# Two spectral filters and a gate in one kernel: weights in freed groups, eight turn buffers, a shorter first fold, and a new order

## The chip, the cores and the metric

The kernel runs on one core of a Trainium2 chip. The metric is the device time of one execution in microseconds, the median of three runs; lower is better. The profile comes from one execution, whose own time is given beside its span.

## The reference

x is 2048 x 1024 in bf16. Two filters work on the same x, each with its own complex weights of 2048 x 513, and a gate per row mixes them:

```python
def reference(A_x, A_w_r, A_w_i, B_x, B_w_r, B_w_i, gate_w):
    # S, D = 2048, 1024
    g = sigmoid((A_x * gate_w).sum(-1, keepdims=True))
    X = rfft2(A_x.astype(float32), axes=(-2, -1))
    a = irfft2(X * (A_w_r + 1j * A_w_i), s=(S, D)).astype(bfloat16)
    b = irfft2(X * (B_w_r + 1j * B_w_i), s=(S, D)).astype(bfloat16)   # the same x
    return g * a + (1 - g) * b
```

B_x is not used. So there is one forward transform, two products with weights, two inverse transforms, and the mix.

## The kernel before

The transforms are written as matmuls with constant matrices. The 2048 rows are split as 128 x 16 (row = 16 n1 + n2), and row n2 of the 16 is one unit of the first and the last steps; the spectrum along the rows is split into 16 groups kg. The steps are:

- **Loads and folds.** x arrives in R1 (`xload`). VectorE folds each row of 1024 by its symmetries into R4. `full_fold` does both levels (a half-length sum and difference, then sum and difference with the reversed half); `half_fold` does one level, and TensorE does the other by accumulating two matmuls, the second with F or with -F (the constant FN).
- **s1(n2)**: the matmuls along n1 with F, 128 columns each. The result is evicted from PSUM to R3 (`evZ`).
- **d(kg), s2(kg), s2x(kg)**: the transform along the 1024 with the constant DM, evicted to QR (`evQ`); then the 16-point step with S2, evicted to XR (`evX`, `evX5`). QR has three slots and XR has four (`NX`).
- **prod(b, m)**: on VectorE, the complex product of X for kg 2m and 2m+1 with the weights of filter b (0 is A, 1 is B), in one of three product tiles. Two instructions multiply (2056 elements each), two instructions combine in place (1028 elements each). For a product named in `DIRECT` the combining instructions are left out, and TensorE combines instead, with four more matmuls for each kg.
- **i1(b, kg)**: the inverse 16-point step with KI, evicted to a buffer of VT (`evV`). Then GpSimd issues a DMA from the VT buffer to R1 (A) or R4 (B), the **turn**, that moves data across partitions; 32 turns in all. The VT buffer comes free when the turn has landed. There are `NV` = 4 buffers. The gate uses parts of VT first, and i1 comes only after `gspec`, the last matmul of the gate's column sum.
- **gmm/gm(c)**: the gate's sigmoid, mixed into the constants of the inverse (RM becomes RA and RB).
- **s1i(n2), di(n2), un(n2), st(n2)**: the inverse along n1 of both filters at once, which needs all 32 turns; eviction `evU`; the inverse along the 1024 with DI; eviction `evo`; four unfold instructions on VectorE; a store.

Each filter's weights are loaded by `wload` in parts of groups kg into WB, which has room for 28 groups (16 of A and 12 of B). The last four groups of B go where A's first four were, after products (0,0) and (0,1). All loads and stores are issued by SP, in one order. Every weight load is written as overwriting the pad columns (`over(["wpad"])`), which the products read, so it waits for the products that were written before it.

The order on every engine is set when the kernel is built. `run` holds lists of units (class `U`), keeps an estimate of when each engine is free and each operand ready (class `Sched`), and takes at each step the unit that can begin first; among those that begin within 40 ns of it, the lowest `prio`. The class waits by semaphores for what is read and overwritten. An eviction goes to ScalarE or VectorE, whichever would end first, with `BIAS` ns in favour of ScalarE when VectorE has other work soon:

```python
ca, cd = 200 + 0.833 * n, 180 + 1.04 * n
ta, td = S.ready("act", self.reads, w), S.ready("dve", self.reads, w)
return (ta, "act", ca) if ta + ca <= td + cd + (BIAS if dnext[0] < td + 400 else 0) else (td, "dve", cd)
```

Of the kernel before, what the change touches and what calls it, by code (L numbers as in the profile page):

```python
# [4 lines left out]
dt = mybir.dt  # L5
# [5 lines left out]
NS = 514  # L11
NX = 4
QUEUE = 2500.0
NV = 4
DIRECT = ((1, 7),)
BIAS = 1200
# [10 lines left out]
def make_consts():  # L27
# [17 lines left out]
    C["FN"] = -C["F"]  # L45
# [89 lines left out]
class Sched:  # L135
# [23 lines left out]
    def op(self, eng, fns, reads=(), writes=(), dma=False, ns=0.0):  # L159
        if not isinstance(fns, (list, tuple)):  # L160
            fns = [fns]
        t0 = self.ready(eng, reads, writes)
        o = Op(eng, len(self.q[eng]), list(fns), dma, len(self.all))
        self.q[eng].append(o)
        self.all.append(o)
        for k in reads:
            assert k in self.writer, k
            o.deps |= self.writer[k]
            o.raw |= self.writer[k]
        for k in writes:  # L170
            if k[0] == "over":
                k = k[1]
            o.deps |= self.writer.get(k, set())
            o.deps |= self.readers.get(k, set())
        writes = [k for k in writes if k[0] != "over"]
        for k in reads:
            self.readers.setdefault(k, set()).add(o)
        for k in writes:
            self.writer[k] = {o}
            self.readers[k] = set()  # L180
        o.deps.discard(o)
        if dma:
            self.free[eng] = t0 + 600 * len(fns)
            self.dmafree = max(self.dmafree, t0) + ns
            o.end = max(self.free[eng], self.dmafree) + 2000
        else:
            self.free[eng] = o.end = t0 + ns
        return o
# [78 lines left out]
def bass_gated_mix__spectral_gfnet__spectral_gfnet__prompt_kernel(  # L267
# [17 lines left out]
    WB = sb("WB", 28 * 2 * NS)  # L285
# [41 lines left out]
    def tt(o, a, b, op):  # L327
        n = int(np.prod(o.shape[1:]))
        return (lambda e: e.tensor_tensor(out=o, in0=a, in1=b, op=op)), 150 + 0.523 * n  # L329
# [9 lines left out]
    class U:  # L339
        def __init__(self, name, eng, ops, reads=(), writes=(), after=(), then=(), prio=5, slot=False, can=None, dma=None):  # L340
            self.name, self.eng, self.ops, self.reads, self.writes = name, eng, ops, list(reads), list(writes)
            self.after, self.then, self.prio, self.slot, self.can, self.dma = after, then, prio, slot, can, dma

        def start(self):

            if any(a not in done for a in self.after) or (self.can and not self.can()):
                return None
            w = self.writes
            if self.eng == "pe" and "m7" in w and mown[0]:
                return None  # L350
            if self.slot:
                best = None
                for s, o in enumerate(psown):
                    if o is None:
                        t = S.ready(self.eng, self.reads, w + [("ps", s)])
                        if best is None or t < best[0]:
                            best = (t, self.eng, s)
                return best
            if self.eng == "ev":
                n = self.n  # L360
                ca, cd = 200 + 0.833 * n, 180 + 1.04 * n
                ta, td = S.ready("act", self.reads, w), S.ready("dve", self.reads, w)
                return (ta, "act", ca) if ta + ca <= td + cd + (BIAS if dnext[0] < td + 400 else 0) else (td, "dve", cd)
            return (S.ready(self.eng, self.reads, w), self.eng, None)
# [50 lines left out]
    def run(streams):  # L415
        streams = [list(s) for s in streams]
        while True:
# [13 lines left out]
            t0 = min(c[0][0] for c in cand)  # L431
            r, u, s = min((c for c in cand if c[0][0] <= t0 + 40), key=lambda c: (c[1].prio, c[0][0]))
# [11 lines left out]

    def xload(a, b):
        return U(("ldx", a), "sp", [(ap(R1, a * 1024, [[1024, b - a], [1, 1024]]), xv[:, a:b, :])], [],
                 [("x", i) for i in range(a, b)], dma=(True, 655.0 * (b - a)))

    def wcol(b, kg):
        return (16 * b + kg) % 28 * 2 * NS  # L450
# [23 lines left out]
    def wload(b, ka, kb, j, c, g0=0, g1=16):  # L474
        key = ("W", b, ka, j, c, g0)
        for k in range(ka, kb):
            wkeys.setdefault((b, k), []).append(key)
        late = (b, ka) == (1, 12)
        u = U(("ldw", key), "sp", wpiece(b, ka, kb, j, c, g0, g1), [], [key] + over(["wpad"] + (wkeys[0, 0] if late else [])),
                 after=[("prod", 0, 0), ("prod", 0, 1)] if late else [], dma=(True, WNS * (kb - ka) * (g1 - g0) / 16.0), prio=6)  # L480
        if b and ka:
            base = u.start

            def start():
                r = base()
                return r and (max(r[0], S.dmafree - QUEUE), r[1], r[2])
            u.start = start
        return u
# [17 lines left out]
    loads = [xload(0, 2), cload("sp", FM, "F", 2048), xload(2, 4), cload("sp", FM, "FN", 2048, at=2048), xload(4, 8), xload(8, 12), xload(12, 16)]  # L506
    w = wseq([(0, 0, 8), (1, 0, 8), (0, 8, 16)], True)
    loads += w[:6] + [cload("sp", DM, "DM", 2048)] + w[6:8] + [cload("sp", S2, "S2", 768)] + w[8:18]
    loads += [cload("sp", KI, "KI", 1280), cload("sp", GS, "GS", 16)] + w[18:] + wseq([(1, 8, 12), (1, 12, 16)])
    lastload = [cload("sp", QR, "DI", 2048, over([("Q", r) for r in range(3)]), after=[("s2", 15), ("s2x", 15)])]  # L510
    midload = [cload("sp", WB, "RM", 2048, over(wkeys[0, 4] + ["wpad"]), after=[("prod", 0, 2)], at=8 * NS)]
# [18 lines left out]
    PEF = (4, 5, 6, 7, 8, 9, 10, 11)  # L530

    def half_fold(n2):

        rd = [("x", n2 + i) for i in range(4)]
        ops = []
        for i, op in enumerate((ALU.add, ALU.subtract)):
            for h in range(2):
                lo = ap(R1, n2 * 1024 + 256 * h, [[1024, 4], [1, 256]])
                hi = ap(R1, n2 * 1024 + 512 + 256 * h, [[1024, 4], [1, 256]])
                o = ap(R4, n2 * 1024 + 512 * i + (511 if h else 0), [[1024, 4], [-1 if h else 1, 256]])  # L540
                ops.append((tt(o, lo, hi, op), rd, [("u", n2 + k, 2 * i + h) for k in range(4)]))
        return U(("fold", n2), "dve", ops, rd, [("u", n2, 0)], after=[("ldx", n2)])

    def full_fold(n2):
        return fold(("fold", n2), 2, R1, n2 * 1024, TR, n2 // 2 % 2 * 2048, R4, n2 * 1024, 0, 128, [("x", n2), ("x", n2 + 1)],
                    ("st", n2 // 2 % 2), [("u", n2), ("u", n2 + 1)], after=[("ldx", {14: 12}.get(n2, n2))])

    folds = [full_fold(0), full_fold(2), half_fold(4), half_fold(8), full_fold(12), full_fold(14)]
    gfold = [fold("gfold", 1, TR, GO, TR, GO + 1024, TR, GO + 2048, 0, 1, ["gw"], ("gst",), [("ug",)], eng="pool", after=[("ld", "gw")])]

    def s1(n2):
        def ops(s):
            r = []
            for q in range(8):
                g, h = q // 2, q % 2
                o, f = pslot(s, q * 128, [[1, 128]]), ap(FM, n2 * 128, [[1, 128]])
                if n2 not in PEF:
                    r.append(mm(o, ap(R4, n2 * 1024 + q * 128, [[1, 128]]), f))
                else:

                    b = n2 * 1024 + g % 2 * 512 + h * 128
                    r.append(mm(o, ap(R4, b, [[1, 128]]), f, True, False))
                    r.append(mm(o, ap(R4, b + 256, [[1, 128]]), f if g < 2 else ap(FM, 2048 + n2 * 128, [[1, 128]]), False, True))
            return r
        return U(("s1", n2), "pe", ops, [("u", n2, i) for i in range(4 if n2 in PEF else 2)] + ["F"] + ["FN"] * (n2 in PEF),
                 after=[("fold", n2 // 4 * 4 if n2 in PEF else n2 // 2 * 2), ("ld", "F"), ("ld", "FN")], slot=True, prio=2,
                 then=[lambda s: EV(("evZ", n2), 1024, ap(R3, n2 * 32, [[512, 32], [1, 32]]), pslot(s, 0, [[32, 32], [1, 32]]),
                                    [], [("Z", n2)], slot=s)])

    def gate_row(c):  # L570

        ops = [mm(ap(PS, 32 * t * 4096 + 7 * 512, [[1, 512]], 0, 32), ap(VT, 2048 + (4 * r + t) * 32, [[1, 32]]),
                  ap(R3, (4 * r + t) * 2048 + c * 128, [[512, 4], [1, 128]]), r == 0, r == 1, 32 * t)
# [18 lines left out]
    allu = [("u", m, i) for m in range(16) for i in range(4 if m in PEF else 2)]  # L592
# [3 lines left out]
    def stage_d(kg):  # L596
        def ops(s):
            return [mm(pslot(s, o, [[1, 256]]), ap(R3, (2 * g + h) * 2048 + kg // 4 * 512 + kg % 4, [[4, 128]]),
# [36 lines left out]
    def prod(b, m):  # L635
# [6 lines left out]
        old = over([("st", i, t) for i in range(2) for t in "ST"] + ["gwt", "F", "FN"])  # L642
# [33 lines left out]
    def stage_i1(b, kg):  # L676
# [22 lines left out]
        def follow(s):  # L699
# [4 lines left out]
            def start():  # L704
                best = None
                for i in range(NV):
                    if vt[i] is None:
                        ev.writes = [("vt", i)] + zr
# [6 lines left out]
            def emit(st):  # L715
# [3 lines left out]
                ev.writes = [("vt", i)] + zr  # L719
# [15 lines left out]
        u = U(("i1", b, kg), "pe", ops, [], after=[("prod", b, kg // 2), "gspec"], can=can,  # L735
# [3 lines left out]
    def gmix(c):  # L739

        ops = [mm(misc(i * 128, [[1, 128]]), ap(ZG, 4 * c + i, [[0, 128]]), ap(WB, 8 * NS + (4 * c + i) * 128, [[1, 128]]))
               for i in range(4)]
        rm = ap(WB, 8 * NS + c * 512, [[1, 512]])
# [23 lines left out]
    def stage_dinv(n2):  # L767
        def ops(s):
            res = []

            for q, o in ((0, 0), (1, 256), (3, 512), (2, 768)):
                for h in range(2):
# [23 lines left out]
                               for t, n, k in ((WB, 56, "wpad"), (XR, 2 * NX, "xpad"))], [], ["wpad"])]  # L796
    run([pads, loads, midload, lastload, aloads, folds, gfold, gate, [s1(n) for n in R16], [stage_d(k) for k in R16], [stage_s2(k) for k in R16],
# [32 lines left out]
```

## Time and profile before

| | |
|---|---|
| median of 3 runs (lowest, highest) | 160.59 us (160.21, 160.77) |
| profiled execution | 159.51 us, span 157.7 us |
| mean granted TensorE clock | 0.941 |
| TensorE busy (1000 matmuls) | 115.1 us, 73% |
| VectorE busy | 114.3 us, 72% |
| ScalarE busy | 102.8 us, 65% |
| GpSimd busy | 25.4 us, 16% |
| moved by DMA | 28.52 MB, mean 181 GB/s |

The span runs from the first to the last instruction; the time of the same execution is 1.8 us longer. Busy times of different engines overlap, so they don't add up. In a group's row the columns are: line, engine, operation, output <- input, shapes and count; then busy time in us and the mean ns of one; then the idle time of the engine just before these instructions, and what ended it. Line 324 is the helper that makes every matmul, line 329 makes every VectorE operation on two tensors, line 374 is an eviction on ScalarE, 376 one on VectorE, and 369 is every DMA, so groups are told apart by their tiles and shapes.

### The profile page before, as it was taken

How to read it: one execution, taken by the hardware profiler on the slowest of the kernel's cores; microseconds unless marked ns; L12 is line 12 of the kernel's file. 1: busy time of each engine (PE TensorE's matmuls, PEld its weight loads, DVE VectorE, ACT ScalarE, POOL GpSimd, SP SyncE). 2: the span in 40 equal slices, each digit the busy share in tenths (PEclk: the TensorE clock that was granted, in tenths of full speed). 3: DMA queues.
4: the chain of work that ended last, by engine and by line, in shares of the span. 5: the costliest groups of instructions: out<-in, count | busy, mean ns of one | idle time of the engine just before them, and what ended most of it. 6: DMA issues, size and time to landing. Idle time of an engine off the chain costs nothing.

```text
span 157.7 us, 2620 instructions
## 1 busy us (share of the span) xinstructions
PE 115.1 (73%) x1000; PEld 79.4 (50%) x1008; DVE 114.3 (72%) x177; ACT 102.8 (65%) x113; POOL 25.4 (16%) x43
## 2 busy tenths in 40 slices
PE   0067999799739747999989964564905999999930
PEld 0054997766413214473635631122305999999920
DVE  0889875469975929399989978995220098998983
ACT  3045599586356526888899994572630688998960
POOL 6900000000003411422404131332310000000000
PEclk9999999999996975999999999999995699999997
DMA  5899999999765897567877857835551005343443
GB/s 151 298 434 422 267 264 244 237 238 217 203 173 117 198 247 142 143 160 194 183 172 153 203 134 186 243 77 152 116 137 50 0 11 192 112 157 137 155 182 133
DMA packets 18478, 28.52 MB, mean 181 GB/s; under 512 B 4641, under 2 KB 12961, under 8 KB 18082
## 3 DMA queue, kind: packets, MB, share of 16 engines
q1 hardware_dynamic: 13712, 19.95, 43.4%
q0 software_dynamic: 4608, 8.41, 23.2%
q8 instruction: 8, 0.13, 0.4%
q14 instruction: 4, 0.03, 0.1%
q10 hardware_dynamic: 146, 0.00, 0.1%
HBM read 15.75 MB, written 4.19 MB: 126 GB/s over the span
## 4 chain that ended last, share of the span: by engine, by line
PE 35%; DMA 21%; DVE 19%; ACT 17%; issue 5%; SPq 1%; DVEq 0%; POOL 0%; ACTq 0%; POOLq 0%
PE PS L324 35%; DMA R<-VT 15%; DVE TR L329 12%; ACT R L374 6%; ACT VT L374 6%; DMA WB<-in_B_w_i_dram 3%; DVE R L329 3%; DMA R<-in_A_x_dram 2%; ACT QR L374 2%; ACT XR L374 2%; DVE FM L329 2%; DVE XR L376 1%; SPq L369 1%; ACT GROW L374 1%; DVE R L376 1%
## 5 line engine op out<-in xcount | busy, mean ns | idle before, releaser
L374 ACT ACTIVATE R<-PS 128x1024 bf16<-128x1024 f32 x43 | 40.8, 1046 | 19.7 <-PE PS L324 19.6
L374 ACT ACTIVATE VT<-PS 128x1024 bf16<-128x1024 f32 (+1 forms) x34 | 32.9, 987 | 18.1 <-DMA R<-VT 14.1
L324 PE MATMUL PS<-TR,KI 128*128 128x512 bf16 x123 | 33.5, 411 | 15.1 <-ACT VT L374 8.4
L329 DVE TENSOR_TENSOR TR<-XR,WB 128x2056 bf16<-128x2056 bf16 x30 | 35.5, 1224 | 8.6 <-PE PS L324 6.1
L324 PE MATMUL PS<-DM,R 128*128 128x256 bf16 (+1 forms) x256 | 33.6, 260 | 1.8 <-ACT VT L374 1.0
L369 POOL DMA_DIRECT2D R<-VT x32 | 19.3, 603 | 89.7 <-ACT VT L374 87.8
L324 PEld LDWEIGHTS PS<-DM,R 128*128 128x128 bf16 x256 | 27.6, 112 | 4.0 <-ACT VT L374 1.9
L329 DVE TENSOR_TENSOR R<-R 128x512 bf16<-128x512 bf16 (+1 forms) x72 | 28.3, 449 | 1.6 <-DMA R<-in_A_x_dram 0.6
L324 PEld LDWEIGHTS PS<-TR,KI 128*128 128x128 bf16 x128 | 11.4, 103 | 31.7 <-ACT VT L374 12.1
L324 PE MATMUL PS<-FM,R 128*128 128x128 bf16 x192 | 15.0, 253 | 9.3 <-DVE R L329 8.9
L324 PE MATMUL PS<-R 128*128 128x128 bf16 x128 | 17.3, 237 | 5.9 <-DMA R<-VT 5.9
L374 ACT ACTIVATE QR<-PS 128x1024 bf16<-128x1024 f32 x15 | 14.9, 1025 | 7.0 <-PE PS L324 7.0
L324 PEld LDWEIGHTS PS<-FM,R 128*128 128x128 bf16 x192 | 14.1, 116 | 10.6 <-DVE R L329 8.8
L324 PE MATMUL PS<-QR,S 128*128 128x511 bf16 (+2 forms) x93 | 16.6, 306 | 2.8 <-ACT VT L374 1.6
L329 DVE TENSOR_TENSOR TR<-TR 128x1028 bf16<-128x1028 bf16 x28 | 18.1, 687 | 0.0
L324 PEld LDWEIGHTS PS<-R 128*128 128x128 bf16 x128 | 13.7, 107 | 6.1 <-DMA R<-VT 6.0
L324 PE MATMUL PS<-QR,R 128*128 128x256 bf16 x128 | 15.0, 273 | 1.3 <-ACT R L374 1.3
L376 DVE CAST R<-PS 128x1024 bf16<-128x1024 f32 x5 | 6.1, 1225 | 12.9 <-PE PS L324 12.9
L324 PEld LDWEIGHTS PS<-QR,S 128*128 128x128 bf16 x96 | 8.5, 98 | 13.2 <-ACT VT L374 2.7
L374 ACT ACTIVATE XR<-PS 128x1024 bf16<-128x1024 f32 (+1 forms) x15 | 11.8, 805 | 4.2 <-DVE FM L329 3.1
L324 PEld LDWEIGHTS PS<-QR,R 128*128 128x128 bf16 x128 | 12.3, 99 | 2.8 <-ACT R L374 1.5
L376 DVE CAST XR<-PS 128x1024 bf16<-128x1024 f32 (+1 forms) x9 | 6.7, 753 | 4.1 <-PE PS L324 4.1
(29 smaller groups left out, 44.8 us busy)
## 6 DMA issues: line engine op xcount, KB each, us to landing
R<-VT POOLq DMA_DIRECT2D x32, 256.0 KB, 5.5
out_dram<-R SPq DMA_DIRECT2D x16, 256.0 KB, 2.0
R<-in_A_x_dram SPq DMA_DIRECT2D x3, 1024.0 KB, 11.4
WB<-in_A_w_r_dram SPq DMA_DIRECT2D x15, 128.2 KB, 4.0
WB<-in_A_w_i_dram SPq DMA_DIRECT2D x13, 128.2 KB, 9.7
WB<-in_B_w_r_dram SPq DMA_DIRECT2D x16, 64.1 KB, 5.2
WB<-in_B_w_i_dram SPq DMA_DIRECT2D x16, 64.1 KB, 4.4
R<-in_A_x_dram SPq DMA_DIRECT2D x2, 512.0 KB, 5.1
```

Source lines behind the costliest of these rows:

```text
L324: return ((lambda e: e.matmul(o, l, r, start=start, stop=stop, skip_group_check=True, **kw)), max(65.0, 0.42 * n) * (1 if tile is None els ...
L329: return (lambda e: e.tensor_tensor(out=o, in0=a, in1=b, op=op)), 150 + 0.523 * n
L369: S.op(eng, [lambda e, d=d, s=s: e.dma_start(d, s) for d, s in self.ops], self.reads, self.writes, dma=self.dma[0], ns=self.dma[1])
L374: S.op("act", lambda e: e.activation(o, i, f), self.reads, self.writes, ns=x)
L376: S.op("dve", lambda e: e.tensor_copy(o, i), self.reads, self.writes, ns=x)
```

## The change

- WB has room for 24 groups. B's groups 8 to 15 go where A's groups 0 to 7 were: 8 to 11 after products (0,0) and (0,1), 12 to 15 after (0,2) and (0,3). The constant RM goes where A's groups 8 and 9 were, after product (0,4), instead of 4 and 5 after (0,2). The hold on late weight loads (`QUEUE`) is taken out.
- VT has 8 buffers. i1 no longer waits for `gspec`; only the three buffers that the gate uses do.
- `DIRECT` has five products instead of one.
- Every row is folded by the new `half_fold`: two instructions that add and subtract the reversed half. In s1 the matmuls have 256 columns: the first of a pair uses F twice, the second F and -F side by side. -F is made from F on ScalarE (`fneg`) instead of loaded.
- F is loaded in two parts, x in eight loads instead of five, and DM and S2 come ahead of all weights.
- The planner's costs, its window (200 instead of 40 ns, within one engine), its priorities (`PRIO`) and `BIAS` (0) are others, and a turn counts as landing 4.2 us after its transfer instead of 2.0.

The diff, cut to its core:

```diff
-QUEUE = 2500.0
-NV = 4
-DIRECT = ((1, 7),)
-BIAS = 1200
+NV = 8
+BIAS = 0
+WIN = 200
+DIRECT = ((0, 1), (1, 6), (1, 1), (0, 7), (1, 4))
+XCH = (0, 1, 2, 4, 6, 8, 12, 14, 16)
+PRIO = {'evU': 6, 'ldw': 2.5, 'gm': 2, 'fold': 0, 'evg': 4, 'evQ': 2.5, 'prod1': 6, 'evV1': 2.5, 's1': 3, 'i11': 1, 's2x': 2, 'di': 3, 'gspec': 1}
...
-    C["FN"] = -C["F"]
...
-            o.end = max(self.free[eng], self.dmafree) + 2000
+            o.end = max(self.free[eng], self.dmafree) + (4200 if eng == "pool" else 2000)
...
-    WB = sb("WB", 28 * 2 * NS)
+    WB = sb("WB", 24 * 2 * NS)
...
-        return (lambda e: e.tensor_tensor(out=o, in0=a, in1=b, op=op)), 150 + 0.523 * n
+        return (lambda e: e.tensor_tensor(out=o, in0=a, in1=b, op=op)), 110 + 0.521 * n
...
-                ca, cd = 200 + 0.833 * n, 180 + 1.04 * n
+                ca, cd = 180 + 0.825 * n, 160 + 1.04 * n
...
-            t0 = min(c[0][0] for c in cand)
-            r, u, s = min((c for c in cand if c[0][0] <= t0 + 40), key=lambda c: (c[1].prio, c[0][0]))
+            t0, e0 = min((c[0][0], c[0][1]) for c in cand)
+            r, u, s = min((c for c in cand if c[0][1] == e0 and c[0][0] <= t0 + WIN), key=lambda c: (c[1].prio, c[0][0]))
...
     def wcol(b, kg):
-        return (16 * b + kg) % 28 * 2 * NS
+        return (16 * b + kg) % 24 * 2 * NS
...
-        late = (b, ka) == (1, 12)
...
-        if b and ka:
-            base = u.start
-
-            def start():
-                r = base()
-                return r and (max(r[0], S.dmafree - QUEUE), r[1], r[2])
-            u.start = start
+        late = (ka - 8) // 4 * 2 if b and ka else None
+        u = U(("ldw", key), "sp", wpiece(b, ka, kb, j, c, g0, g1), [], [key] + over(["wpad"] + (wkeys[0, 0] if late is not None else [])),
+                 after=[("prod", 0, late), ("prod", 0, late + 1)] if late is not None else [], dma=(True, WNS * (kb - ka) * (g1 - g0) / 16.0), prio=6)
...
+    xl = [xload(a, b) for a, b in zip(XCH, XCH[1:])]
+    loads = [fload(0)] + xl[:3] + [fload(1)] + xl[3:] + [cload("sp", DM, "DM", 2048), cload("sp", S2, "S2", 768)]
     w = wseq([(0, 0, 8), (1, 0, 8), (0, 8, 16)], True)
-    loads += w[:6] + [cload("sp", DM, "DM", 2048)] + w[6:8] + [cload("sp", S2, "S2", 768)] + w[8:18]
+    loads += w[:18]
...
-    midload = [cload("sp", WB, "RM", 2048, over(wkeys[0, 4] + ["wpad"]), after=[("prod", 0, 2)], at=8 * NS)]
+    midload = [cload("sp", WB, "RM", 2048, over(wkeys[0, 8] + ["wpad"]), after=[("prod", 0, 4)], at=16 * NS)]
...
+    def half_fold(n2, n):
+        rd = [("x", n2 + i) for i in range(n)]
+        ops = []
         for i, op in enumerate((ALU.add, ALU.subtract)):
...
+            ops.append((tt(ap(R4, n2 * 1024 + 512 * i, [[1024, n], [256, 2], [1, 256]]), ap(R1, n2 * 1024, [[1024, n], [512, 2], [1, 256]]),
+                           ap(R1, n2 * 1024 + 511, [[1024, n], [512, 2], [-1, 256]]), op), rd, [("u", n2 + k, i) for k in range(n)]))
...
+    folds = [half_fold(a, b - a) for a, b in zip(XCH, XCH[1:])]
+    fneg = [U(("FN", c), "act", [((lambda e, c=c: e.activation(ap(FM, 2048 + c * 512, [[1, 512]]), ap(FM, c * 512, [[1, 512]]), ACT.Copy, scale=-1.0),
+                                   610.0), [("F", c > 0)], [("FN", c)])], [("F", c > 0)], [("FN", c)], after=[("ld", ("F", c > 0))], prio=0) for c in range(4)]
...
+            for t in range(2):
+                for h in range(2):
+
+                    o, b, f = pslot(s, t * 512 + h * 256, [[1, 256]]), n2 * 1024 + t * 512 + h * 128, n2 * 128
+                    r.append(mm(o, ap(R4, b, [[1, 128]]), ap(FM, f, [[0, 2], [1, 128]]), True, False))
+                    r.append(mm(o, ap(R4, b + 256, [[1, 128]]), ap(FM, f, [[2048, 2], [1, 128]]), False, True))
...
                     if vt[i] is None:
-                        ev.writes = [("vt", i)] + zr
+                        if i < 3 and "gspec" not in done:
+                            continue
+                        ev.writes = [("vt", i)] + (zr if i < 3 else [])
...
-        u = U(("i1", b, kg), "pe", ops, [], after=[("prod", b, kg // 2), "gspec"], can=can,
+        u = U(("i1", b, kg), "pe", ops, [], after=[("prod", b, kg // 2)], can=can,
```

## The prediction

> **What bounds the kernel now.** I read the page first, then the busy time by stretches of ten microseconds, then the chain, the waits, the groups by shape, and the DMA issues with their landings. The chain gives the stages:
>
> ```profile
> 0.74 3.63 DMA R<-in_A_x_dram
> ...
> 14.51 12.68 PE PS L324 x175
> ...
> 51.84 7.38 DMA R<-VT
> ...
> 74.93 4.88 DMA WB<-in_B_w_i_dram
> ...
> 95.86 7.17 DMA R<-VT
> ...
> 105.38 5.62 DMA R<-VT
> ...
> 115.98 4.11 DMA R<-VT
> 120.10 0.05 issue
> 120.14 23.83 PE PS L324 x288
> ```
>
> Columns: start, duration, what (us). Opening: x arrives, is folded, goes through TensorE until 28.5. Middle: from 28.5 to 120.1, spectra, products, inverse along q2, and the "turns" (DMA R<-VT), which appear four times on the chain. End: from 120.14, when the last turn has landed, 35 us of inverse matmuls, evictions and unfolds. The waits say who stands still for the turns:
>
> ```profile
> ACT VT L374 <- DMA R<-VT: 14.1, 8, 2.6
> ...
> PE PS L324 <- DVE R L329: 8.9, 1, 8.9
> ```
>
> ScalarE waited 14.1 us in 8 pieces for one of the four VT buffers to come back; TensorE's first wait, 8.9 us, is for the first fold. The stretches show what the waits cost:
>
> ```profile
> core 0: us, PE busy (x) PEld busy (x) DVE busy (x) ACT busy (x) POOL busy (x), PEclk, DMA share, GB/s
> ...
> 50.00:60.00 10.00, 6.24 (x22) 1.76 (x20) 6.59 (x9) 4.68 (x5) 3.00 (x5) 0.84 0.90 202
> ...
> 70.00:80.00 10.00, 9.45 (x60) 5.24 (x60) 9.06 (x13) 8.89 (x10) 2.99 (x5) 1.00 0.78 187
> 80.00:90.00 10.00, 9.54 (x63) 5.57 (x63) 9.90 (x11) 9.39 (x12) 2.39 (x4) 1.00 0.73 173
> ...
> 100.00:110.00 10.00, 4.75 (x23) 1.75 (x23) 8.82 (x11) 4.75 (x5) 2.39 (x4) 1.00 0.59 145
> 110.00:120.00 10.00, 3.82 (x19) 1.68 (x20) 1.70 (x4) 3.94 (x5) 2.39 (x4) 0.92 0.50 125
> ```
>
> From 70 to 90 three engines are over 88% busy: that is this stage without turn waits. At 50 to 60 and after 100 they are half idle: that is the room. The end (130 to 140: PE 10.00, DVE 9.40, ACT 9.43) is full, and nothing there shrinks.
>
> **The change, part by part.** Durations by group:
>
> ```profile
> L329 DVE TENSOR_TENSOR TR<-XR,WB 128x2056 bf16<-128x2056 bf16 x30 | 35.5, 1224 | 8.6 <-PE PS L324 6.1 <-DMA WB<-in_B_w_i_dram 1.1 <-ACT XR L374 1.1
> ...
> L329 DVE TENSOR_TENSOR TR<-TR 128x1028 bf16<-128x1028 bf16 x28 | 18.1, 687 | 0.0
> ```
>
> *Folds.* Before: groups of 8 instructions each at 6.1, 6.0 and 5.0, so 17.1 us of VectorE. After: 16 instructions, four of 512 elements (0.42, the row of 512-element unfolds), ten of 1024 (0.684, the half folds of before), two of 2048 (1.22, the nearest product row): 1.7 + 6.8 + 2.4 = 10.9, a saving of 6 us. The reversed operand needs no surcharge: the old second step reads reversed too and ran 1.29 for two. GpSimd's gate fold covers 2.21 to 7.64; the first two VectorE folds took 2.25 for the pair against 1.28 later. The Trainium skill (SBUF — State Buffer, "SBUF: two separate sides") calls the shared port an exclusive lock: each early fold would wait out a 1.36 us GpSimd instruction, some 4 us for the first three rows; the row gives a slowing of 1.8, 1.5 us. I take the row.
>
> *First-stage matmuls.* 192 of 128 columns become 128 of 256 columns. The former took 14.5 us as issued (the timeline's runs); stage d's 24 matmuls of 256 columns took 2.79, 0.116 each, so 14.9. A moving operand that reads F twice is not in the trace: at no penalty +0.4, at half speed +15; I take +0.4, since it is contiguous in runs of 128 like the others.
>
> *-F and x.* -F is not loaded (0.5 MB) but made by four ScalarE copies of 512 at 0.60, 2.4 us: the first before ScalarE's first eviction (it sat idle 6.96 us), the others beside evictions; at worst 1.8 us. F's first quarter, x row 0 and smaller loads come first: TensorE starts at about 5.5 instead of 8.85. With 16 x 0.93 and three gate rows at 0.62 the stage ends near 22.5, not 28.5. SP issues 12 loads ahead of the weights instead of 7, DM and S2 now among them (stage d wants them sooner; the bytes ahead of A's last lower weight stay the same, -F apart). In all the opening has three issues more: 1.6 us of SP at 0.5 each, against 1.9 us less DMA (0.5 MB at some 270 GB/s).
>
> *What is late next.* The first product needs X (34.2 now, about 28.8 after) and A's lower weights, landed at 30.3 now. The second of m = 0 needs B's:
>
> ```profile
> WB<-in_B_w_i_dram SPq DMA_DIRECT2D x1, 16.0 KB, 4.2
> ```
>
> issued by 36.4, landed at 40.6. The XR ring holds X for four kg, and X 4 is overwritten only after both products of m = 0. So of the 6 us won, about 2.5 remain: product (1,0) starts at 40 instead of 42.5. The early i1 (no longer behind the gate's last matmul, 42.25) fills the gap on TensorE.
>
> *Direct products.* Four more of 16: 8 VectorE instructions fewer at 0.646, 5.2 us; 32 more matmuls of 512 columns at 0.21 (1.68 for 8), 6.7 us of TensorE. TensorE was 95% busy in the good stretch, so between 5.2 gained and 1.5 lost; I count half, 2.6.
>
> *Eight turn buffers.* In the good stretch products start at 70.58, 75.74, 79.89, 84.70, 88.19: 4.40 apart. Over all 13 from 42.54 to 105.70 it is 4.86. At 4.40, less 2.6 in all: 40 + 57.2 - 2.6 = 94.6 for the last product's start. Turns take 0.60 of POOL each and landed in 4.1 to 8.1; eight in flight share DMA engines that the turns fill for 23.2% of the span, 1.14 us each, so a bunch of eight drains in 9, as fast as ScalarE fills it.
>
> *B's upper weights.* They now lie in A's groups: kg 8 to 11 after products (0,0) and (0,1), kg 12 to 15 after (0,2) and (0,3); the planner's hold is gone. Each load also waits for the products written before it (they read the pad columns), as now:
>
> ```profile
> SPq L369 <- DVE TR L329: 22.6, 10, 4.7
> ```
>
> The 32 loads went out from 48.0 to 93.7, 1.44 each. RM (0.3 to issue, 6.4 to land) now waits for (0,4) instead of (0,2); its first reader came at 89.1, so a product or two of delay stays hidden, and its place in SP's queue costs the loads behind it that wait if it is written in too early. DI goes last, as now. At the same pace from 47, the last goes at 93 less little, lands by 4.4 (page), and (1,6), 2.4 long as a direct product, must precede (1,7): start near 95.8 if the pace is a bit better, 99 if not. I take 95.8, the later of this and 94.6.
>
> *From the last product to the end stage.* Now 105.70 to 120.14, 14.4 us, turn waits in it. After: product 3.66, two i1 1.9, eviction 1.0, turn 0.6 and landing 4.1: 11.3, less a little overlap, 11. The end stage starts at 106.8: 13.3 earlier.
>
> *End stage.* BIAS 0 and the priorities move evictions between ScalarE (0.96 each back to back) and VectorE (1.22). VectorE has 64 x 0.366 = 23.4, and the balance is at 3 evictions, what it has now. Bounds -1.5 and +3; I take 0. TensorE begins it at half clock (granted 0.50 from 120 to 124, full again past 126) after 5.85 us idle, and will again. The skill (TensorE: Matmul & The Clock Gate, "The HAM clock gate") has the clock back after about 3.4 us of activity, which would cost 1.7 us; the row shows over 5 us, 2.6. Either is in both kernels. In the middle 10.2 us ran at half clock (47 to 65), up to 5 us; by the rule the gaps of over 3.4 us alone bring it, and only the wait for B's lower weights threatens one. I count no gain.
>
> **Sum.** -2.5 opening, -10.8 middle (pace, direct products, shorter drain), 0 end: -13.3. The profiled execution took 159.51, span 157.7 and 1.8 around it, 1.1 under the median 160.59; its span should become 144.4. Against the median: 147.3.
>
> **Rivals.**
> *Weights replace turns (0.24).* The pace stays 4.86 since PSUM's three slots, the XR ring or SP's loads set it. For: VectorE waited for B's weights at 79.9 and 98.7 already. Against: only 1.1 us of it. 40 + 63.2 + 11 = 114.2, 5.9 earlier: 154.7.
> *All savings land (0.14).* VectorE bounds, direct products bring 5.2, no weight is late: 40 + 52 + 11 = 103, end -1.5: 142.
> *Slower: B's upper weights starve (0.10).* VectorE gets denser, a load goes out only in a gap between products, 32 in-order loads sit behind them, and every product of m = 4 and 6 waits. It decides when the last lands after 106.7 (then the last product starts at 109.1 and the end stage at 120.1): 1.75 us per load from 47, against 1.44. At 2.0 the last lands at 115.4, 8.7 later: 169.
> *It does not do what it says (0.02).* The order written out by other costs puts turns no closer, and the gains cancel: 160.6.
>
> **Numbers.** The forecast, 144 to 151, has 0.50; all savings 0.14, weights 0.24, slower 0.10, no change 0.02. From 142 to 155 leaves out half of the best case, the slower one and no change, about 0.19. Faster by more than 0.3% (0.5 us, about what a measurement of this kernel tells from no change) 0.88, within it 0.02, slower 0.10.
>
> **What would show it.** ScalarE's wait for R<-VT near zero; first matmul near 5.5; fold groups near 11 us; first 128x256 of stage d near 23; (1,0) near 40; the x288 run starting near 107; SP's loads ended before 92. Wrong, if a wait of DVE for WB loads of several microseconds appears, if the 256-column matmuls take over 0.15 each, or if VectorE's casts of 1024 rise from 12 to over 25.

## The result, and the profile after

The changed kernel took 152.37 us (149.25 to 155.65, 4 runs) against 160.4 for the kernel before: a ratio of 0.938, 95% interval 0.925 to 0.952. A second set of six runs gave 151.69 against 160.01, ratio 0.952 (0.948 to 0.956). Executions of one kernel differ here by up to 4%, so each ratio is taken from the executions within 1.5% of the fastest of their kernel, while a median in us is taken from all of them, and the two need not agree. The forecast was 147.3, within 142 to 155: the direction was right, and so was the fall of the waits for turns, but by the two profiled executions only 8.1 us of the 13.3 came.

The profiled execution took 151.47 us with a span of 149.6, which is 8.1 less than before. First the stretches of ten microseconds, with the columns as before (busy time of PE, PEld, DVE, ACT and POOL, granted clock, DMA share, GB/s):

```profile
core 0: us, PE busy (x) PEld busy (x) DVE busy (x) ACT busy (x) POOL busy (x), PEclk, DMA share, GB/s
...
50.00:60.00 10.00, 9.87 (x58) 5.17 (x57) 8.25 (x10) 6.69 (x8) 3.51 (x6) 1.00 1.05 205
...
70.00:80.00 10.00, 7.31 (x41) 3.66 (x40) 8.18 (x10) 6.61 (x7) 2.60 (x5) 1.00 0.69 164
...
90.00:100.00 10.00, 5.35 (x23) 2.09 (x23) 5.36 (x5) 4.44 (x5) 2.39 (x4) 0.95 0.89 240
100.00:110.00 10.00, 7.26 (x36) 3.23 (x34) 5.29 (x8) 5.44 (x6) 2.38 (x4) 0.84 0.47 106
110.00:120.00 10.00, 7.77 (x82) 6.98 (x81) 3.03 (x7) 5.07 (x6) 0.00 (x0) 0.69 0.14 42
```

The hole at 50 to 60 is gone (TensorE 9.87 instead of 6.24, at full clock instead of 0.84), and the end stage begins inside the last stretch. A new hole stands at 90 to 100, where all three engines are half idle. The waits name what fills it; columns: waiting engine, who ended the wait, us in total, times, longest:

```profile
DVE TR L330 <- DMA WB<-in_B_w_i_dram: 4.0, 1, 4.0
...
ACT VT L377 <- DMA R<-VT: 3.3, 2, 1.9
```

ScalarE's wait for turns fell from 14.1 to 3.3, as forecast. VectorE's wait for B's weights rose from 1.1 to 4.0, all in one piece. SP's own waits:

```profile
SPq L372 <- DVE TR L330: 16.8, 11, 3.1
```

SP still stood behind products 11 times: the weight loads wait, and then a product waits for them. The chain of work that ended last (start, us, what) shows both that and the opening:

```profile
4.50 2.68 DVE R L330 x2
...
7.22 3.42 PE PS L325 x16
...
10.66 1.22 DVE R L379
...
47.25 7.75 DMA R<-VT
...
64.85 7.16 DMA R<-VT
...
91.65 5.33 DMA WB<-in_B_w_i_dram
...
99.53 5.07 PE PS L325 x16
...
107.87 5.20 DMA R<-VT
...
113.12 21.92 PE PS L325 x280
```

Turns are on the chain three times instead of four. The wait for B's weights ends at 97.0. After it TensorE needs 5.07 us for 16 matmuls of 512 columns, 0.32 each instead of 0.21, because its granted clock has dropped to half. The stretch from 100 to 101, with the columns as above:

```profile
100.00:101.00 1.00, 1.00 (x4) 0.35 (x3) 1.00 (x2) 0.00 (x0) 0.00 (x0) 0.50 0.96 189
```

The end stage starts at 113.12 instead of 120.14.

The gain by stage is the same sum as in the forecast. Product (1,0) starts at 39.81 instead of 42.54: 2.7. The last product starts at 99.30 instead of 105.70: 3.7 more. From there to the end stage 13.8 instead of 14.4: 0.6. The end stage takes 36.5 instead of 37.6: 1.1. Together 8.1.

### The profile page after: what moved, and what is told of

Its sections match the earlier page's. It is cut to its first block, busy times and chain, and to the rows that moved or that the text cites. A ratio compares the mean times of both kernels' runs of the same rounds, so it can differ in the third digit from the quotient of the medians.

```text
span 149.6 us, 2547 instructions
## 1 busy us (share of the span) xinstructions
PE 119.2 (80%) x968; PEld 80.2 (54%) x976; DVE 110.6 (74%) x167; ACT 100.0 (67%) x111; POOL 24.7 (16%) x43
## 4 chain that ended last, share of the span: by engine, by line
PE 46%; DMA 19%; DVE 16%; ACT 7%; issue 6%; SPq 2%; DVEq 0%; POOL 0%; POOLq 0%; ACTq 0%
PE PS L325 46%; DMA R<-VT 13%; DVE R L330 8%; DVE TR L330 6%; ACT VT L377 4%; DMA WB<-in_B_w_i_dram 4%; ACT R L377 3%; SPq L372 2%; DMA R<-in_A_x_dram 2%; DVE R L379 2%; POOL R L372 0%; DVEq L246 0%; DVEq L232 0%; DVE XR L379 0%; DVE VT L379 0%
## 5 line engine op out<-in xcount | busy, mean ns | idle before, releaser
L377 ACT ACTIVATE VT<-PS 128x1024 bf16<-128x1024 f32 (+2 forms) x33 | 30.7, 960 | 22.1 <-PE PS L325 18.7
L325 PE MATMUL PS<-TR,KI 128*128 128x512 bf16 x147 | 36.7, 391 | 7.9 <-DVE TR L330 5.3
L330 DVE TENSOR_TENSOR R<-R 128x512 bf16<-128x512 bf16 (+2 forms) x80 | 35.2, 496 | 5.6 <-DMA R<-in_A_x_dram 4.5
L330 DVE TENSOR_TENSOR TR<-XR,WB 128x2056 bf16<-128x2056 bf16 x28 | 33.0, 1223 | 6.0 <-DMA WB<-in_B_w_i_dram 4.0
L325 PE MATMUL PS<-DM,R 128*128 128x256 bf16 (+1 forms) x256 | 31.7, 251 | 0.9 <-ACT R L377 0.6
L325 PEld LDWEIGHTS PS<-TR,KI 128*128 128x128 bf16 x152 | 14.0, 99 | 27.5 <-issue 5.7
L325 PE MATMUL PS<-FM,R 128*128 128x256 bf16 x128 | 16.2, 289 | 8.9 <-DVE R L330 8.9
L379 DVE CAST R<-PS 128x1024 bf16<-128x1024 f32 x7 | 8.6, 1223 | 10.4 <-PE PS L325 10.4
L330 DVE TENSOR_TENSOR TR<-TR 128x1028 bf16<-128x1028 bf16 x18 | 11.6, 687 | 0.0
L379 DVE CAST XR<-PS 128x4 bf16<-128x4 f32 (+1 forms) x12 | 8.3, 696 | 3.1 <-PE PS L325 3.0
```

The costliest lines, as they stand in the source:

```text
L325: return ((lambda e: e.matmul(o, l, r, start=start, stop=stop, skip_group_check=True, **kw)), max(65.0, 0.42 * n) * (1 if tile is None els ...
L377: S.op("act", lambda e: e.activation(o, i, f), self.reads, self.writes, ns=x)
L379: S.op("dve", lambda e: e.tensor_copy(o, i), self.reads, self.writes, ns=x)
```

## The experiments

**The changed kernel again**, as reference on the chip of the next two and of "Four buffers, planned anew". The other kernels below ran on another chip, without the changed kernel beside them; they are compared with it by their ratios to the kernel before.

> The changed kernel once more, as the reference for its neighbours on this chip: about 151 to 153 us, ratio 0.93 to 0.96 to the kernel before. Both theories expect the wait of VectorE for B's weights, 4 us near 93 to 97, and the granted clock at a half soon after it.

151.69, ratio 0.952 (0.948 to 0.956). In its trace VectorE's wait for B's weights is 2.1 us instead of the expected 4, ScalarE's for turns 6.4, and the expected half clock doesn't come: the granted clock is 1.00 from 90 to 108. The last product starts at 99.68, no sooner than in the first execution. So how the missing time is split between the two varies between executions, and so does the total: the kernel's runs spread over 4% in the first set, those of the kernel before over under 1%.

**The loads' extra waits taken away, order kept.** The pad column is written by a memset and read by products, but the weight loads don't write it. In the edit a key marked "plan" counts for the planner as before, but leaves behind only the wait for the memset. The order on all five engines is unchanged.

```diff
-[key] + over(["wpad"] + (wkeys[0, 0] if late is not None else []))
+[key] + [("plan", "wpad")] + over(wkeys[0, 0] if late is not None else [])
...
+            o.deps |= self.writer[k[1]] if k[0] == "plan" else set()
```

> The changed kernel with the order on every engine left as it is; only the waits of the weight loads (and of RM) for the products written before them, which come from the pad columns, are left out. The real waits stay: for the first write of the pads, and of B's upper half for the products that read A's lower groups. Theory W (the loads' extra waits make B's last weights late): SP's waits for VectorE shrink from 19 us to a few, the last B weight is issued before 75 instead of 92.3, the 4.05 us wait of VectorE is gone, and with it the half clock after it: 4 to 6 us less than the changed kernel, 146 to 148. Rival D (the DMA engines are full, 1.05 busy from 50 to 70): the earlier loads only take the turns' place there, the median landing of a turn rises from 6.5 to 8 or more, ScalarE waits for turns again, and the time stays within 1 us of the changed kernel.

149.87, ratio 0.935 (0.930 to 0.941): by the ratios 1.8% or 2.7 us better than its neighbour (1.8 us by the medians), about half of what theory W said and more than D allowed. SP's waits, ScalarE's for turns, and the time from issue to landing of the turns, in its profiled execution, which took 151.62 us:

```profile
SPq L372 <- DVE TR L330: 13.4, 2, 10.2
SPq L372 <- PE PS L325: 9.4, 1, 9.4
```

```profile
ACT VT L377 <- DMA R<-VT: 7.9, 4, 3.4
```

```profile
DMA to landing us min/median/max: 4.4/6.4/10.4
```

Instead of 11 waits for products SP has one among the weight loads, 10.2 us, until A's groups have been read; the 9.4 us are DI's wait for the matmuls of the forward transform, and the rest is RM's. The last B weight is issued at 82.6 instead of 92.3, and no product waits for weights any more: the last product starts at 97.68 instead of 99.30. The half clock stays, now from about 90.5 to 93.9, after a gap of 2.32 us on TensorE. ScalarE waits 7.9 us for turns, not much over the 6.4 of the neighbour, and the median landing of a turn is 6.4 us, so D's sign, 8 or more, did not come.

**The same, planned anew.** The planner is told that the loads don't wait for products.

```diff
-[key] + over(["wpad"] + (wkeys[0, 0] if late is not None else []))
+[key] + over(wkeys[0, 0] if late is not None else [])        # and "wpad" as a read
```

> As the kernel without the loads' waits for products, but the planner knows it and writes another order: the gate's first sigmoids and mixes come before the last products instead of after them. Theory W: the same 4 to 6 us, and 1 to 3 us more because the gate's four links (106 to 113 now) are partly out of the time between the last product and the end stage: 144 to 147. Rival D: within 1.5 us of the changed kernel.

148.19, ratio 0.926 (0.921 to 0.931): by the ratios 2.8% or 4.2 us under the changed kernel beside it (3.5 us by the medians), more than rival D allowed and less than theory W's 5 to 9. **It is the fastest kernel of the study that does the whole work.** In its trace no product waits for weights, and ScalarE doesn't wait for turns at all, although the DMA engines are full for 40 us:

```profile
core 0: us, PE busy (x) PEld busy (x) DVE busy (x) ACT busy (x) POOL busy (x), PEclk, DMA share, GB/s
...
50.00:60.00 10.00, 9.94 (x58) 5.47 (x58) 8.54 (x10) 6.93 (x8) 3.44 (x6) 1.00 1.10 195
...
70.00:80.00 10.00, 9.08 (x49) 4.46 (x49) 9.97 (x12) 7.30 (x8) 3.24 (x6) 1.00 1.08 219
80.00:90.00 10.00, 8.66 (x54) 4.55 (x52) 8.06 (x13) 8.55 (x10) 2.39 (x4) 1.00 1.06 195
```

```profile
DMA to landing us min/median/max: 4.2/8.6/11.4
```

The second view is that of the turns: their median landing is 8.6 us, 5.5 before and 6.5 after. Rival D's sign is there, but eight buffers cover it in this order. The last product starts at 94.99, 4.3 us sooner than in the changed kernel. From there to the end stage it still takes 14.3 us: moving the gate's links brought nothing that shows in that stretch, and TensorE enters it at half clock (about 92.8 to 96.2), after a gap of 2.42 us that was no wait for weights.

**Half of the late bytes**, on top of the first of these two.

```diff
-        n = src.shape[-1]
+        n, w = src.shape[-1], 256 if b and ka else src.shape[-1]
...
-[1, n]]), ... [1, n]]
+[1, w]]), ... [1, w]]
```

> The kernel with the changed kernel's order and without the loads' waits for products, with one thing more left out: of B's weights for kg 8 to 15 only 256 of the 513 columns are loaded, so half of their bytes (1 MB), with the same instructions. The other columns hold what lay there before. Rival D in its present form (without the extra waits the loads fill the DMA engines, turns land later, and ScalarE's four waits for turns, 7.9 us, eat half of the gain): turns land sooner, ScalarE's wait for them falls below 4 us, and the time is 146 to 148.5. If the DMA engines are not what delays the turns: the waits stay and the time is 149 to 151.

148.29, ratio 0.918 (0.902 to 0.934) on another chip.

```profile
ACT VT L377 <- DMA R<-VT: 3.3, 2, 2.9
```

The median landing falls from 6.4 to 5.7 and ScalarE's wait from 7.9 to 3.3, as rival D said. But two executions of the changed kernel itself had 3.3 and 6.4, so one trace proves little. The time's interval overlaps that of the kernel with all bytes (0.930 to 0.941), so the price of the full DMA engines lies anywhere from nothing to some 6 us there. The size stays open.

**Four buffers, planned anew.**

```diff
-NV = 8
+NV = 4
```

> The changed kernel with four turn buffers instead of eight, planned anew. If the eight buffers carry the gain of the middle (the forecast: ScalarE's wait for turns, 14.1 us before, 3.3 after, and the pace of products 4.86 to about 4.3 us), the wait is back at over 10 us and the time is 157 to 161. If they carry little and the gain is from the fold and the direct products, 152 to 154.

162.33, ratio of the medians 1.015: over the expected range, though the fastest of its four executions, 159.09, lies within it. But its planner wrote another order on four engines, so this number holds two things. Hence:

**Four buffers, order kept.** The planner runs once with eight buffers; its list of steps, with engine, PSUM slot and product tile of each, is then written out with four.

```diff
-    S = Sched() ... run([...])
+    plan(NV, DIRECT, None, tiles, trail)                  # as in the changed kernel
+    S = plan(4, DIRECT, list(trail), tiles, [])           # the same steps, four buffers
```

> The changed kernel with four turn buffers, but with the changed kernel's order on every engine kept as it is (before the gate's last matmul only one buffer is free of the gate, instead of five). Theory O (a buffer is worth most through the order that it allows; eight buffers let this order run): in this order the ScalarE evictions wait for turns one by one, over 20 us of such waits, and the time is 163 to 175, no better than the four-buffer kernel with its own order (162.3). Rival (the loss of that kernel came from its other order alone): within 3 us of the changed kernel.

159.97, ratio 0.987 (0.977 to 0.996). Neither side had it: far over "within 3 us", and under the 163 that the first named.

```profile
ACT VT L378 <- DMA R<-VT: 18.7, 7, 5.5
```

With VectorE's part 23.7 us of waits for turns (in an execution of 161.45 us), as the first said, yet by the ratios the time is only 3.5 to 5% over that of the changed kernel, 5 to 8 us. Most of it comes early. The fourth product, in the changed kernel and here:

```profile
44.61 2.37 DVE L330 TENSOR_TENSOR FM<-XR,WB 128x2056 bf16<-128x2056 bf16 x2
```

```profile
52.23 2.37 DVE L331 TENSOR_TENSOR FM<-XR,WB 128x2056 bf16<-128x2056 bf16 x2 [7.46 <-ACT XR L378]
```

7.6 us are lost by then, while the gate still holds three buffers and only one is free instead of five. From there to the last product it takes 56.5 us here and 54.7 in the changed kernel, of which 2.4 and 4.0 are waits for B's weights. So the edit changes two things, the number of buffers and how many of them are free of the gate, and in this trace the second costs more.

**The buffers alone**, in the kernel before (WB of 24 groups, NV 8, i1 free of `gspec`), with the old planner and its hold on late loads (`QUEUE`).

```diff
-NV = 4
+NV = 8
-    WB = sb("WB", 28 * 2 * NS)
+    WB = sb("WB", 24 * 2 * NS)
...
-        late = (b, ka) == (1, 12)
+        late = (ka - 8) // 4 * 2 if b and ka else None
```

> The kernel before with one part of the change: B's upper weights in A's groups, WB of 24 groups, eight turn buffers, i1 free of the gate's last matmul. Folds, loads of x, direct products and planner stay as before. Theory W (the buffers bring the middle's gain): ScalarE's wait for turns falls from 14 us to under 5, and the time to 152 to 155. Rival (the part only works with the new order and folds): within 2 us of the kernel before, 158 to 162.

167.19, ratio 1.049 (1.035 to 1.062): slower, outside both expectations. ScalarE's wait for turns did fall, from 14.1 to 7.2. SP's last group of loads, and the product that waits for it:

```profile
96.24 7.38 SPq L369 DMA_DIRECT2D WB<-in_B_w_i_dram  x3
```

```profile
109.82 2.37 DVE L329 TENSOR_TENSOR TR<-XR,WB 128x2056 bf16<-128x2056 bf16 x2 [4.79 <-DMA WB<-in_B_w_i_dram]
```

The three loads stand behind DI in SP's order and go out until 103.6; the product before the last starts at 109.82. That is the forecast's slower rival at work: "It decides when the last lands after 106.7". SP waits 29.0 us for products here, 22.6 before. It comes out where the planner puts the loads badly. What the hold adds to it was not tested apart.

**All parts, old planner.**

```diff
-BIAS = 0
+BIAS = 1200
...
-            self.prio = PRIO.get(kind, prio)
+            self.prio = prio
...                                          # and the old costs and window
```

> The changed kernel's buffers, folds and direct products, but with the planner's costs, window, priorities and bias of before, so another order. If the order carries a good part of the gain (the forecast put none of it there): 155 to 160. If the buffers and folds carry it: 150 to 154.

164.01, ratio 1.026 (1.019 to 1.034): slower than the kernel before, over the whole expected range.

```profile
ACT VT L377 <- DMA R<-VT: 11.6, 7, 3.5
```

With eight buffers and the old planner's order ScalarE still waits 11.6 us for turns, and VectorE 5.7. Why the kernel is slower than the one before, where ScalarE waited 14.1, is not shown.

**The new planner alone**, on the buffers, folds and direct products of before.

```diff
-BIAS = 1200
+BIAS = 0
+WIN = 200
+PRIO = {...}                                # as in the change, with the new costs
```

> The kernel before with the new planner alone: its costs, window, priorities and bias 0; buffers, folds, loads and direct products as before. Theory P (the priorities only fit the eight buffers and new folds, and four buffers still hold ScalarE up): 158 to 165, ScalarE's wait for turns at 8 us or more. Rival (the order alone gives the gain): 151 to 156.

159.33, ratio 0.987 (0.979 to 0.995), and ScalarE waits 7.4 us for turns: theory P by the time, and nearly by the wait (8 or more). The new planner is worth 1% on the old parts, and the parts cost 3 to 5% with the old planner. Only together do they give 5 to 6%.

**One direct product**, planned anew, and with the order kept (the same replay as above).

```diff
-DIRECT = ((0, 1), (1, 6), (1, 1), (0, 7), (1, 4))
+DIRECT = ((1, 7),)
```

> The changed kernel with only product (1,7) direct, as before; planned anew. VectorE gets 8 combining instructions more (0.65 each, 5.2 us), TensorE 32 matmuls of 512 columns fewer (0.21 each, 6.7 us). Theory V (VectorE sets the middle's pace, so four direct products bring about 2.6 us, as the forecast counted): 153 to 156. Rival T (TensorE sets the pace, 94 to 99% busy from 40 to 70): the same as the changed kernel or up to 2 us less, 149.5 to 152.

159.67, ratio 0.987 (0.976 to 0.999): above the range of either side, and the trace says why.

```profile
DVE TR L330 <- DMA WB<-in_B_w_i_dram: 10.0, 2, 6.5
```

In the other order weights come late by 10 us (in an execution of 161.75 us); on direct products it says nothing.

> The changed kernel's order kept, with only product (1,7) direct: eight combining instructions of VectorE come back in their places, 5.2 us, and 32 matmuls go. Planned anew, this kernel took 159.7, with 10 us of waits for B's weights in it. If the direct products themselves are worth the forecast's 2.6 us: 153 to 156. If all of VectorE's 5.2 us show: 156 to 158. If TensorE sets the pace: 150 to 152.5, and the 159.7 came from the other order alone.

152.52, ratio 0.936 (0.927 to 0.944), on another chip than the changed kernel's 0.952, and no worse than its first 0.938.

```profile
PE PS L326 <- DVE TR L331: 12.1, 7, 3.1
```

In this execution (154.41 us) TensorE waits 12.1 us for products instead of 5.3, 6.8 more, about the 6.7 us of matmuls that it no longer has. The two kernels did not run side by side, and the four further direct products are worth nothing that this comparison can tell.

**The gate's fold on VectorE**, in the order of the fastest kernel.

```diff
-[("ug",)], eng="pool", after=[("ld", "gw")])]
+[("ug",)], eng="dve", after=[("ld", "gw"), ("fold", 2)])]
```

> The fastest kernel so far (loads without waits for products, 148.2), its order kept, with one move: the gate's fold (four operations on one partition) goes from GpSimd, where it runs from 2.1 to 6.9, to VectorE after the fold of rows 2 and 3. Theory L (VectorE's first folds wait out GpSimd's instructions: 2.68 us for the first pair of 512 elements, against 0.4 each elsewhere): the first pair takes under 1.0, the first matmul starts at 5.5 instead of 7.2, and 0.5 to 1.5 us come off the time, less 1.5 us that VectorE now spends on the gate: 146.5 to 148.5. Rival (the first folds are slow for another reason, x or F arriving, or the shape): the first pair stays over 2 us and the time is 148.5 to 150.

150.17, ratio of the medians 0.933 against 0.926 on another chip, and the fastest executions 147.60 and 146.72: no gain shown. The start is as theory L said (timeline, VectorE and TensorE):

```profile
4.91 0.76 DVE L331 TENSOR_TENSOR R<-R 128x512 bf16<-128x512 bf16 x2 [4.91 <-DMA R<-in_A_x_dram]
...
5.73 3.60 PE L326 MATMUL PS<-FM,R 128*128 128x256 bf16 x16 [5.73 <-DVE R L331]
```

The first pair of folds takes 0.76 instead of the 2.24 of the kernel in whose order it runs (2.68 in the changed kernel), and the first matmul starts at 5.73 instead of 7.34. But those 16 matmuls take 3.60 all the same, then TensorE waits for the gate's column (1.04), and stage d starts only 0.76 sooner. In the middle of this execution (150.23 us) ScalarE waited 5.1 us for turns where the other kernel had none. That this is where the 0.76 went is not shown.

## Why the prediction was right, and where it was off

**The range, right; the figure, not quite.** The medians, 152.37 and 151.69, lie within 142 to 155 but outside the 144 to 151 that the forecast gave to its own path, and nearer to the rival "Weights replace turns" (154.7, chance 0.24) than to 147.3. By mechanism the result stands between the two: the waits for turns fell as forecast, and weights came in their place late in the middle. The forecast's own sign of being wrong, a wait of VectorE for loads to WB of several microseconds, was there: 4.0.

**Turn buffers, right, but not in full for its reason.** The forecast said that four buffers hold the middle up. With the order kept, four instead of eight cost 5 to 8 us, most of it while the gate still held three of them. The forecast gave the early i1 no time of its own: it only "fills the gap on TensorE". The pace of products was forecast from the good stretch, 4.40 less 0.2, so 4.20. It measures 4.58 from 39.81 to 99.30, and 4.26 with the one 4.05 us wait taken out. So the pace was right to 2% where no weight was late, and 9% too fast as it came.

**B's upper weights, the wrong end taken.** The step "start near 95.8 if the pace is a bit better, 99 if not. I take 95.8" failed: the last product started at 99.30. Its own terms, 93 less a little, 4.4 and 2.4, make 99, and it gave no number for the better pace that should bring 95.8. The last load went out at 92.3, as forecast ("93 less little"), and landed by 97.0. The cause is shown: without the extra waits of the loads no product waits for weights, and the time falls by 2.7 us in the same order and 4.2 in an order made for it. The wait is not all of it: with a wait of 2.1 instead of 4.0 the second execution reached the last product at 99.68, after more waiting for turns.

**From the last product to the end stage, too small.** The sum "product 3.66, two i1 1.9, eviction 1.0, turn 0.6 and landing 4.1" measured 13.8 instead of 11. The term forgot the product before: its 16 matmuls began at 99.53, at half clock after TensorE's 2.86 us of idle time, and ended at 104.4, when the last product had been ready since 102.9. The last turn landed in 5.2 instead of 4.1. In the second execution, at full clock, the same stretch took 12.8, so the clock's part is about 1 us. The forecast's rule for the clock, "the gaps of over 3.4 us alone bring it", did not hold: half clock came with gaps of 2.86 us here and 2.42 and 2.32 in the two kernels without the extra waits, and did not come with one of 2.90 before 75.67 in the second execution. A sooner turn alone would have helped by 1.54 us at most: the gate's mixing matmuls, ahead of the end stage in TensorE's order, ended at 111.58, and the end stage began at 113.12.

**Opening, right by accident.** "TensorE starts at about 5.5" was 7.22. I weighed the lock on the port that GpSimd and VectorE share against a slowing of 1.8, and took the slowing. The pair of 512 took 2.68, against 0.76 with GpSimd free: for this row the lock was the nearer of the two. GpSimd was done at 6.87, so only this row met it: the first six folds took 4.70 us, against 2.72 with GpSimd free, 2.0 more, where the forecast had 1.5 for the slowing and 4 for the lock. The stage then ended near 26.4 instead of 22.5, and stage d began at 26.96, only 1.5 us sooner than before. Two evictions of 1.22 went to VectorE between folds, with BIAS 0, and stand on the chain at 10.66 and 15.10. The first 16 matmuls took 3.42 where 16 later ones took 1.92. So the first product started at 32.70 instead of 28.8. Product (1,0) at 39.81 looks like the forecast's 40, but not by its reason, B's weights: VectorE was busy right up to it. The folds' sum was close, 12 us against 10.9, and 256 columns cost 0.112 each at full clock (64 in 7.16), so reading F twice carries no penalty.

**Direct products, none seen instead of 2.6.** Where VectorE and TensorE are both near full, moving work from one to the other moved nothing that these ratios can tell (0.936 with one direct product, 0.938 and 0.952 with five, not measured side by side).

**End stage, 1.1 instead of 0**, inside the bounds given.

**What the forecast did not have: the order as a term of its own.** It gave the new planner no gain and no loss, apart from evictions. It was luck that the order was a good one: the forecast had no reason for it. With the old planner's order the same parts took 164, outside its range.

## What to carry to other kernels

Where every queue runs in a fixed order, a part's worth is not a number of its own: test it once with the order kept and once planned anew, or the planner's luck (here 5% for the direct products, 8% for all parts) passes for the part's effect. Look for waits that only the bookkeeping makes, such as a load that waits for readers of a column that it doesn't write; before the change they cost little, 1.1 us of products waiting for B's weights, and after it 4.0 and 2.1. When a stall goes, price the next one with the clock and with the backlog that it leaves on the engine behind it.

## What was not expected of the hardware

- One VectorE instruction of 512 elements took 1.38 us while GpSimd ran instructions of 1.19 us on one partition, and the pair took 2.68 against 0.76 without them. The size of the GpSimd operand (one partition of 128) did not spare VectorE.
- The granted clock stands at 1.00 in the profile's rows from the start, but the first 16 matmuls of 256 columns took 0.21 each and later ones 0.12 or less, as at half clock. Starting 1.6 us sooner did not shorten that: 3.60 us for the 16 with the gate's fold on VectorE and without.
- Half clock came with a gap of 2.32 us on TensorE in one trace and not with one of 2.90 in another. The length of a gap alone did not tell.
- With weight loads and turns together, in the fastest kernel, the DMA engines were 1.06 to 1.10 busy for 40 us while they moved only 195 to 219 GB/s; in the opening, with x, they moved over 400 in the best slices.
